# Score tiles of 40 columns, Wo products that may run as column pairs, and a new order of TensorE's pieces

## The chip, the core and the metric

One core of a Trainium2 chip runs the whole program. The metric is device time in microseconds (us), the median of several executions. Three executions of the kernel before took 2647.1, 2651.34 and 2651.9 us.

## What is computed

Two layers in turn, each an attention with a recurrent memory (A) and a gated feed-forward (B), on 2048 tokens of width 576:

```python
x = x + A(layernorm(x)); x = x + B(layernorm(x))     # layer 0
x = x + A(layernorm(x)); x = x + B(layernorm(x))     # layer 1, the same weights

# A: 64 segments of 32 tokens; the 8 memory rows come from the segment before
h = concatenate([mem, xs])                 # 40 x 576
q, k, v = h @ Wq, h @ Wk, h @ Wv           # 32 heads of 128
p = softmax(where(mask, q @ k.T * scale, -1e9))   # 40 x 40 for each head
o = concat_heads(p @ v) @ Wo               # 40 x 576
mem = o[:8]; out = o[8:]

# B
out = (silu(x @ w1) * (x @ w3)) @ w2       # hidden width 4608
```

## The kernel before

The weights of A stay in SBUF. The program walks through 72 steps. In step t, layer 0 works on segment t and layer 1 on segment t-8, so in most steps (56 of 72) each product of A streams 80 columns, 40 for each layer; in the steps at the two ends only one layer is there, and 40 columns are streamed. The feed-forward of a group of four segments is spread over the following four steps, since A alone is a chain from one segment to the next.

`make_nodes` writes all this down as pieces ("nodes"), and `plan` puts them in order. A step has four groups of eight heads. For each group stand, in order of what they need: QK and QKt (the projections to q and k; QKt is the tail of the contraction, 64 rows), SC (scores), the softmax on VectorE and ScalarE, TR (the probabilities transposed, by a DMA where two layers are there), PV (probabilities times V), OTe (its result copied to OT), WO (OT times Wo, four blocks of 128 output columns for each head: 32 products) and WOt (the last 64 columns: 8 products). VG and VGt make V. FF and FFt are w1 and w3, W2 and W2b are w2.

The order of the pieces on TensorE (PE) is a string of letters, `FIRST + FOUR * 11 + LAST` (S is SC, O is WO, o is WOt, and so on); `FOUR` holds four steps and stands eleven times. The other engines' orders follow from due times.

Each piece has a way to use the array of 128 x 128: "full", "col" (products with 64 or 40 output rows, two side by side in the two halves of the columns), "row" (contraction of 64, two above each other), and narrower strips for some of V. A piece may allow several ways, written "full/col". `plan` keeps the way of the piece before as long as the new piece allows it, and counts a change of way otherwise (about 0.096 in its table). Where a "full/col" piece falls into a column stretch, `mm` (line 729's helper) writes each of its products as two with 64 output rows:

```python
def mm(self, out, lhsT, rhs, start, stop, **k):
    if self.mode == "col" and "tile_position" not in k:
        for r in (0, R64):
            self.mm(out[r:r + R64], lhsT[:, r:r + R64], rhs, start, stop, tile_position=(0, r), **k)
        return
```

Each product is a weight load (LDWEIGHTS, PEld in the profile) and a MATMUL. In `scores`, a group with two layers has eight products for the first layer in one half of the columns and eight for the second in the other. The first layer's use 64 columns of weights (40 of its own and 24 of the neighbour), the second's 40.

Of the kernel before, what the change touches and what calls it, by code (L numbers as in the profile page):

```python
# [13 lines left out]
P = 128  # L14
R64 = 64
# [6 lines left out]
QW = SEG + MEM  # L22
# [45 lines left out]
def role(t):  # L68

    return (t - LAG) % 2  # L70
# [152 lines left out]
def ew(*ns):  # L223
    return (actc(*ns), dve(*ns))


def ewh(*ns):
# [2 lines left out]


FIRST = (
    "maqqQQQqSSvxVTXTqPQPSXSOOTPooOoTxPOoQqQSqqqSQQSSvTTVPTPOPoOTOPooOoQqqQvSSVqQQSqSTTPPOOoToTPaPOOooQqvqqSQVSQTQSqx"
    "PTSOPXOTToPoPOOooQqqpvSQVSnqQFFTSfqfPTQFOSPWTFOPoffTOPFOoooWQqfqQSFSVvqfqQQFTTSWPPFSOOxffXToFPWoTfOPFOooFQfqfqQS"
    "VqqvSQQSWTFSPTFfPOTOoPfWTOPFOoooFQffqqQSWQSqVvTSFfQqfWFSTafPFPOToWPTOPOOooobQqqqpQQQxSnXFvqfVSFfqqQQFfqSQPWQqfOS"
    "FPXxWOooPffFFPOOooWQQQqqfqFSFqfqQQQSFqqqfQQWFggfSGSGPGPgfFOOoPWGgfOPFOoooWFqqfQQFSqfqQQQSFvfqqQVSqWqQQfPPSFfOOWP"
    "FOfoFPaooOoWQQqqqqQSQQbSqqqQGSgQqPQGggSPGGPgOOOoPooOoQqqvpQpQQnSqqVqnSQFffqFQQPQqqfSFSOPWwfFOooFPfOWPwfFOooFqqfq"
    "QQQSqqqQQQSWwFfGSFqqfgQQPwWgSGFPGgfOOPWgfGFOoPOoooaqqQQQQqqwFfSSVvQQqqfFWSPwFqfqQQPFSwfOWOFPffFOwWoPOoooFfqqqQQW"
    "SQQqqqQSbQGSgqqQPQGSgOPGggOPGwOoPooOo"
)  # L240
FOUR = (
    "QqqqppQQvVSnnQFqfqqQQSFSFfqfqQQwWPFfPOOSWFoPowffFFPOOoowWQQfqfqFSFfqqqQQwQWSFgfqqQGQPQqgfSWSGFPOwoGggGPOPOOoooaF"
    "qfqqQQQSFqqqfQQQwWvSSVFPQFffqqQOPSWwoffFOPFOwPWOoooFqfqqQQWQSQqqqQQSwSbQQqgqgGSGPGPOoggGPOPOOooo"
)
LAST = (
    "QqqqppQQQqSvVSnnQQqqfFSqqQPQFSffOPFOwPWFOfFoPoofOoWQQQqqqwSQFQqqfGSqgQQPQqfSFGgqgPGSWwfFOFPOfgGOwoPOoooqqqQQQQqS"
    "WFfSVvqfqQFQQPWSwFqfqfQPFOSwWOPFffFOWwoPOoooFqqfqQQQSQFQqqfqQSVSvqqQQWwfSPFVvPWOwPOOobPooxOoXqpQpQqqvVSnSnQFFSTf"
    "fqPTQFSwFPWOTTffPOPOOooooFqffqQQSwFWSQvVqqQTSFPSTWPwFOTffTPOPOOoooowFWvxXVfqQQqfqSQSFFfqSQTwTSWPPFOffTOPFWTOFPwO"
    "ooooFfqfqQQSFSQwfqqQSWSVvTTFwWPffFPOTOTPWPOOoooowbqqpQQxvSSnXVFQfqqQTSTFfSPFPOwTOPFffooTOPFOoowQfqqqQSQSFvVTSQqf"
    "XPFSTwPOTffFPOTFPOOoooofxQfqqQSFSvVwTQqqFSffQwPTSFTPFPOffOTOPwOooooFQqQSqqvVSQQSqwTTSFPFPOoTOoTPffPOOoopfwfFFnFw"  # L250
    "fffFFFwffFFwfffFFwFwfffFFFwffFFwffFFwfffFFww"
)
ORDER = FIRST + FOUR * 11 + LAST

# [1 line left out]
class Opt:  # L256

    qk, qkt, sc, tr, pv, wo, wog, vm = 0.0079, -0.0342, 0.0268, 0.1447, 0.0406, 0.2653, 0.0725, 0.1407
# [4 lines left out]
def make_nodes(em, nseg, pools, o=Opt, dma_bw=230e3, load_bw=380e3, tail_bw=330e3):  # L263
# [4 lines left out]
    def node(*a, **k):  # L268
        n = Node(*a, **k)
        n.prio += 1e-9 * len(nodes)  # L270
        nodes.append(n)
        return n

    def banks(n=2):
        return [Slot("bank") for _ in range(n)]
# [7 lines left out]
    def both(t):  # L283

        return len(layers_of(t - role(t))) == 2


    def load(name, nbytes, prio, fn, deps=()):
        return node("DMA", nbytes / (tail_bw if name == "tail" else load_bw), fn, deps=deps, prio=prio, name=name, lat=2.0)
# [6 lines left out]
    ld_o = [load("ldo", kb(n * E, 576), g - 6.0, em.load_o(g)) for g, (_, n) in enumerate(GROUPS)]  # L296
# [93 lines left out]
    def step(t):  # L390
        ls = layers_of(t)
        nl = 2 if both(t) else 1
# [4 lines left out]
        mm80 = max(c80 / 2.4 + 2.7, 25.1) / 1000  # L397
# [13 lines left out]
        for g, (h0, nh) in enumerate(GROUPS):  # L411
            qs, qe = [], []
            for uh, un in units(g, nl):
# [4 lines left out]
                if pre:  # L418
                    xl.append(node("DMA", 0.5, em.xq_load(t, uh, q), deps=[v[0] for v in [kept_qk.get((t // 4, uh // 4))] if v] + last_qk[-BACK:][:1], prio=pq - 0.3, acq=[q], lat=2.6, name="XL", ring=1.3))
                m_ = node("PE", 8 * un * mmq, em.qk(t, uh, un, b), deps=hx + hm[:1] + ([ld_h[g]] if t == 0 else []),  # L420
                          prio=pq, mode="full", acq=[q] + b, name="QK")
                last_qk.append(m_)
                n = node("PE", un * mmq, em.qk_tail(t, uh, un, b), deps=hx + hm + ([ld_h[g]] if t == 0 else []), prio=pq + o.qkt, mode="row",
                         acq=[q] + b, name="QKt")
                rd += [m_, n]
                me.setdefault(f"QK{g}", []).extend([m_, n])
                for r in (0, 1):
# [4 lines left out]
            s = banks(1)[0]  # L432
            sme = Slot("sme")
            pf = t + o.gstep * h0 / 8
            w40 = nh * QW
            sc = node("PE", nh * (0.0155 * nl if nl == 2 else 0.0255), em.scores(t, g, qs, s), deps=qe, prio=pf + o.sc, mode="col" if nl == 2 else "full/col",
                      acq=[s, sme], rel=[q for q, _, _ in qs], name="SC")
            a = node("DVE", dve(w40), em.sm_add(t, g, s, sme), deps=[sc], prio=pf, rel=[s], name="add")
            m_ = node("DVE", dve(w40, w40) + 0.13, em.sm_max(t, g, sme), deps=[a], prio=pf, name="maxsub")
# [14 lines left out]
            if paired(t):  # L454
                hn = [ht_ready[li, s] for s in (t + 1, t + 2) for li in (0, 1) if (li, s) in ht_ready]
                for blk in blks:
                    if blk // 2 not in vgs:
# [4 lines left out]
            ot = [Slot("ot") for _ in range(nl)]  # L462
            pv = node("PE", nh * mm80, em.pv(t, g, pts, b), deps=pe_ + [d for blk in blks for d in vx_ev["VM", t, blk] + vx_ev["VX", t - e, blk]],
                      prio=pf + o.pv, mode="full/col", acq=b + ot, rel=[pts], name="PV")
            pvs[t, g] = pv
            if paired(t):
                for blk in blks:
                    gb, gd = vgs[blk // 2]
                    vx_ev["VX", t + 1, blk] = vg_out(t, blk, gb, gd + [pv], 0)
            ote = [node("AD", ew(w40), em.ot_ev(t, g, ab, b[ab], ot[ab]), deps=[pv], prio=pf, rel=[b[ab]], name="OTe") for ab in range(nl)]  # L470
            wo = node("PE", 4 * nh * mm80, em.wo(t, g, ot), deps=ote + ([ld_o[g]] if t == 0 else []), prio=t + o.wo + o.wog * h0 / 8, mode="full",
                      acq=[y] if g == 0 else [], name="WO")
            wot = node("PE", nh / 2 * mm80 + (0.013 if nl == 2 else 0.04), em.wo_tail(t, g, ot), deps=[wo], prio=t + o.wo + o.wog * h0 / 8, mode="col", rel=ot[g == NG - 1:], name="WOt")
            if g:
# [11 lines left out]
        if nxt:  # L486
            m = 8 * len(nxt)
# [191 lines left out]
    for t in range(nst):  # L679
        if t % 4 == 2 and (t + 2) // 4 < ngrp:  # L680
            x_in((t + 2) // 4)
        if t == LAG:
            ht_mem[t].append(node("DVE", 0.1, em.init_mem(1, LAG), deps=[m0e] + reads_ht.get(LAG - R_HT, []), prio=LAG - 2, name="m0"))
        if role(t) == 0 or t == 0:
            vx_pair(t - role(t), t - 1 + o.vx)
        step(t)
        if t % 4 == 1 and t // 4 < ngrp:
            x_res(t // 4)
        if t % 4 == 3:
            job((t + 1) // 4 - 1)  # L690
        elif t == nst - 1:
            job(nst // 4)
# [12 lines left out]
class Emitter:  # L705
# [482 lines left out]
    def scores(self, t, g, qs, s):  # L1188

        def f(n):  # L1190
            nh = GROUPS[g][1]
            S = self.bk(s)[:, 0:nh * QW].rearrange("p (h k) -> p h k", h=nh)
            both = self.both(t)
            w = QW * self.nl(t)
            for i in range(max(un for _, _, un in qs)):
                for q, j0, un in qs:
                    if i >= un:
                        continue
                    Q = self.T.QKT[:, q.i]
                    for kd in ((0, 1) if both else (0,)):  # L1200
                        m = (R64 if kd == 0 else QW) if both else P if n.mode == "full" else QW
                        q0 = i * w + (QW * (kd ^ role(t)) if both else 0)
                        self.mm(S[64 * kd:64 * kd + m, j0 + i, :], Q[:, q0:q0 + m], Q[:, un * w + q0:un * w + q0 + QW],
                                True, True, **({"tile_position": (0, 64 * kd)} if n.mode == "col" else {}))
        return f
# [414 lines left out]
```

## Time and profile before

| what | value |
|---|---|
| three executions | 2647.1, 2651.34, 2651.9 us |
| span of the profiled execution | 2659.8 us |
| mean granted TensorE clock | 0.990 |
| instruction count of the profiled execution | 132,078 |
| DMA moved | 371.41 MB |

The profiled execution's own span is 8.5 us (0.3%) above the median of the three. Times inside the program, such as "1450.34", are microseconds from the start of that span. In rows of the timeline the first number is the start, the second the length from the first start to the last end, and "x32" the number of merged instructions; in rows of groups the number behind the bar is the group's share of the engine's busy time in us, and the next the mean length of one instruction in ns. Matmuls overlap in the pipeline, so that length is longer than the distance from one to the next.

### The profile page before, as it was taken

How to read it: one execution, taken by the hardware profiler on the slowest of the kernel's cores; microseconds unless marked ns; L12 is line 12 of the kernel's file. 1: busy time of each engine (PE TensorE's matmuls, PEld its weight loads, DVE VectorE, ACT ScalarE, POOL GpSimd, SP SyncE). 2: the span in 40 equal slices, each digit the busy share in tenths (PEclk: the TensorE clock that was granted, in tenths of full speed). 3: DMA queues.
4: the chain of work that ended last, by engine and by line, in shares of the span. 5: the costliest groups of instructions: out<-in, count | busy, mean ns of one | idle time of the engine just before them, and what ended most of it. 6: DMA issues, size and time to landing. Idle time of an engine off the chain costs nothing.

```text
span 2659.8 us, 132078 instructions
## 1 busy us (share of the span) xinstructions
PE 2571.8 (97%) x58776; PEld 2214.4 (83%) x58818; DVE 2045.3 (77%) x5137; ACT 1225.1 (46%) x3495; POOL 336.9 (13%) x399
## 2 busy tenths in 40 slices
PE   5899999999999999999999999999999999999998
PEld 4778887888888888888888888888888888888887
DVE  4777777777878778788777878877787788778876
ACT  2545453444545354454535444453544445344453
POOL 1111111011101111010111111011110111011110
PEclk8899999999999999999999999999999999999999
DMA  9045746565554655545465555546555554554457
GB/s 317 9 144 155 188 99 142 125 145 146 106 141 115 164 135 147 134 118 139 113 156 126 150 130 129 132 113 152 126 151 133 136 137 105 121 148 120 132 162 246
DMA packets 690428, 371.41 MB, mean 140 GB/s; under 512 B 234328, under 2 KB 682592, under 8 KB 689216
## 3 DMA queue, kind: packets, MB, share of 16 engines
q1 hardware_dynamic: 686320, 355.08, 52.6%
q8 instruction: 460, 7.54, 1.2%
q0 software_dynamic: 3024, 6.93, 1.0%
q10 hardware_dynamic: 512, 0.94, 0.1%
q14 instruction: 112, 0.92, 0.1%
HBM read 306.72 MB, written 2.36 MB: 116 GB/s over the span
## 4 chain that ended last, share of the span: by engine, by line
PE 85%; DMA 6%; DVE 5%; issue 1%; ACT 1%; SPq 0%; ACTq 0%; POOL 0%; DVEq 0%; POOLq 0%
PE bank L729 85%; DMA PTS<-PB 2%; DMA W<-in_B_w_dram 2%; DVE STAT L735 1%; DVE V L735 1%; DVE SME L735 1%; DVE PB L735 1%; DMA W<-in_A_Wq_dram 1%; DMA WO<-in_A_Wo_dram 0%; DMA W<-in_A_Wk_dram 0%; DVE HTT L735 0%; ACT V L732 0%; DVE XR L735 0%; DMA WV<-in_A_Wv_dram 0%; SPq L738 0%
## 5 line engine op out<-in xcount | busy, mean ns | idle before, releaser
L729 PEld LDWEIGHTS <-W 128*128 128x128 bf16 (+2 forms) x31872 | 1258.3, 100 | 150.0 <-issue 72.7
L729 PE MATMUL bank<-HT,W 128*128 128x80 bf16 (+3 forms) x23040 | 796.8, 197 | 23.6 <-issue 8.7
L729 PE MATMUL bank<-XTB,W 128*64 128x256 bf16 (+5 forms) x8832 | 667.4, 263 | 9.2 <-DMA W<-in_B_w_dram 5.8
L1264 POOL MEMSET PB<- 128x1024 bf16 x288 | 273.3, 953 | 1764.3 <-DMA PTS<-PB 1066.0
L732 ACT ACTIVATE QKT<-bank 128x128 bf16<-128x128 f32 (+2 forms) x1497 | 356.0, 316 | 276.9 <-PE bank L729 269.2
L729 PE MATMUL bank<-OT,WO 128*128 128x80 bf16 (+3 forms) x11520 | 414.3, 199 | 5.9 <-ACT OT L732 3.1
L729 PEld LDWEIGHTS <-WO 128*128 128x128 bf16 (+1 forms) x11520 | 385.9, 102 | 22.9 <-issue 10.8
L732 ACT ACTIVATE V<-bank 32x512 bf16<-32x512 f32 (+1 forms) x563 | 319.7, 585 | 174.5 <-PE bank L729 163.1
L729 PE MATMUL bank<-WV,HT 128*32 128x512 bf16 (+4 forms) x3735 | 366.0, 387 | 9.2 <-DMA WV<-in_A_Wv_dram 4.4
L729 PE MATMUL bank<-W2C,HTT 128*64 128x288 bf16 (+1 forms) x3136 | 317.2, 287 | 0.2 <-DMA W2C<-in_B_w_dram 0.2
L732 ACT ACTIVATE HTT<-bank 128x512 bf16<-128x512 f32 (+1 forms) x324 | 176.0, 550 | 277.9 <-PE bank L729 275.4
L735 DVE TENSOR_REDUCE STAT<-SME 104x8 f32<-104x320 f32 (+1 forms) x576 | 274.8, 477 | 29.9 <-ACT SME L732 20.3
L735 DVE TENSOR_TENSOR PB<-SME,STAT 40x128 bf16<-40x128 f32 (+4 forms) x912 | 275.3, 336 | 12.0 <-POOL PB L1264 1.0
L729 PEld LDWEIGHTS <-HT 128*32 128x32 bf16 (+5 forms) x3776 | 157.8, 101 | 139.6 <-issue 42.4
L735 DVE SCALAR_TENSOR_TENSOR HTT<-HTT,bank 128x512 bf16<-128x512 bf16 (+1 forms) x324 | 201.6, 622 | 82.3 <-ACT HTT L732 78.8
L732 ACT ACTIVATE SME<-SME 104x320 f32<-104x320 f32 (+1 forms) x288 | 135.5, 471 | 280.6 <-DVE SME L735 276.9
L729 PEld LDWEIGHTS <-HTT 128*64 128x64 bf16 (+1 forms) x3216 | 232.2, 105 | 32.6 <-issue 1.2
L735 DVE SCALAR_TENSOR_TENSOR XR<-bank,XR 128x288 f32<-128x288 f32 x574 | 240.6, 448 | 16.2 <-PE bank L729 11.8
L732 ACT ACTIVATE OT<-bank 128x320 bf16<-128x320 f32 (+2 forms) x430 | 164.1, 401 | 184.9 <-PE bank L729 171.9
L735 DVE CAST V<-bank 64x512 bf16<-64x512 f32 (+1 forms) x301 | 206.4, 686 | 43.4 <-PE bank L729 35.6
L735 DVE TENSOR_TENSOR HTT<-HTT,bank 128x512 bf16<-128x512 bf16 (+1 forms) x324 | 203.6, 628 | 28.1 <-PE bank L729 0.5
L735 DVE CAST QKT<-bank 128x192 bf16<-128x192 f32 (+4 forms) x423 | 124.4, 335 | 114.3 <-PE bank L729 111.3
(59 smaller groups left out, 1396.5 us busy)
## 6 DMA issues: line engine op xcount, KB each, us to landing
W<-in_B_w_dram SPq DMA_DIRECT2D x608, 256.0 KB, 3.7
W2C<-in_B_w_dram SPq DMA_DIRECT2D x304, 288.0 KB, 3.4
W<-in_B_w_dram SPq DMA_DIRECT2D x608, 32.0 KB, 3.3
W<-in_B_w_dram SPq DMA_DIRECT2D x16, 512.0 KB, 7.3
WO<-in_A_Wo_dram SPq DMA_DIRECT2D x4, 1152.0 KB, 9.8
XR<-in_A_x_dram POOLq DMA_DIRECT2D x16, 288.0 KB, 3.0
WV<-in_B_w_dram SPq DMA_DIRECT2D x8, 576.0 KB, 6.5
W<-in_A_Wq_dram SPq DMA_DIRECT2D x16, 256.0 KB, 7.1
```

The costliest lines, as they stand in the source:

```text
L729: self.ch("PE", self.nc.tensor.matmul(out, lhsT=lhsT, rhs=rhs, start=start, stop=stop, skip_group_check=True, **k))
L732: self.ch("ACT", self.nc.scalar.activation(*a, **k))
L735: self.ch("DVE", getattr(self.nc.vector, fn_)(*a, **k))
L1264: return lambda n: self.ch("POOL", self.nc.gpsimd.memset(self.T.PB[:, pb.i, 0:GROUPS[g][1]], 0.0))
```

## The change

Three edits, none of which changes what is computed.

1. `scores`: both layers' products use 40 columns of weights. The planner's figure for a group falls from 0.0155 to 0.0126 for each head and layer.
2. WO allows "full/col" in place of "full" where two layers are there.
3. `FIRST`, `FOUR` and `LAST` are new strings with the same letters in each in another order (a line of `FOUR` is shown).

```diff
@@ -230,25 +230,25 @@
 FOUR = (
-    "QqqqppQQvVSnnQFqfqqQQSFSFfqfqQQwWPFfPOOSWFoPowffFFPOOoowWQQfqfqFSFfqqqQQwQWSFgfqqQGQPQqgfSWSGFPOwoGggGPOPOOoooaF"
+    "QqqqppQQVvnSnQFqqqfQQSFSFfqqfQQPWFwSffPOFOwWooffFPFPOOoowQQQqqqqSQWSFfqqqQQQQFqfgfFSGwWPFgfSGGPOoggwOPGWPOOoooFq"
...
@@ -433,7 +433,7 @@
-            sc = node("PE", nh * (0.0155 * nl if nl == 2 else 0.0255), em.scores(t, g, qs, s), deps=qe, prio=pf + o.sc, mode="col" if nl == 2 else "full/col",
+            sc = node("PE", nh * (0.0126 * nl if nl == 2 else 0.0255), em.scores(t, g, qs, s), deps=qe, prio=pf + o.sc, mode="col" if nl == 2 else "full/col",
...
@@ -468,7 +468,7 @@
-            wo = node("PE", 4 * nh * mm80, em.wo(t, g, ot), deps=ote + ([ld_o[g]] if t == 0 else []), prio=t + o.wo + o.wog * h0 / 8, mode="full",
+            wo = node("PE", 4 * nh * mm80, em.wo(t, g, ot), deps=ote + ([ld_o[g]] if t == 0 else []), prio=t + o.wo + o.wog * h0 / 8, mode="full/col" if nl == 2 else "full",
...
@@ -1198,7 +1198,7 @@
-                        m = (R64 if kd == 0 else QW) if both else P if n.mode == "full" else QW
+                        m = P if n.mode == "full" and not both else QW
```

Counted over the whole program, the pieces and their products are the same, but more of them run in column pairs: of the 7,168 full WO products with 80 columns 480 are left, and 13,376 halves stand for the others. PV has 336 full products in place of 1,256, w2 616 in place of 1,328, w1 and w3 2,032 in place of 2,976 (with 256 columns). In all PE has 9,423 matmuls more, each with its weight load, 68,241 in place of 58,818. One copy of `FOUR` has 3,994 matmuls in place of 3,314. The way of using the array changes 1,097 times over the program, before 1,171 times.

The first place is on PE, in the middle of the program, where the scores of a group begin (QKT is q and k of the group, W and HT the projection ahead of it, W2C and HTT a w2 product ahead of it). Before:

```order
L729 LDWEIGHTS W
L729 MATMUL bank_92<-HT,W 128x80
L729 LDWEIGHTS QKT
L729 MATMUL bank_89<-QKT 64x40
L729 LDWEIGHTS QKT
L729 MATMUL bank_89<-QKT 40x40
L729 LDWEIGHTS QKT
L729 MATMUL bank_89<-QKT 64x40
```

And in the changed kernel:

```order
L729 LDWEIGHTS HTT
L729 MATMUL bank_87<-W2C,HTT 128x288
L729 LDWEIGHTS QKT
L729 MATMUL bank_90<-QKT 40x40
L729 LDWEIGHTS QKT
L729 MATMUL bank_90<-QKT 40x40
L729 LDWEIGHTS QKT
L729 MATMUL bank_90<-QKT 40x40
```

The number of products is the same; the ones with 64 output rows are gone.

The second place is on PE too, where WO follows a PV in column pairs. Before:

```order
L729 MATMUL bank_92<-PTS,V 64x80
L729 LDWEIGHTS V
L729 MATMUL bank_92<-PTS,V 64x80
L729 LDWEIGHTS WO
L729 MATMUL bank_90<-OT,WO 128x80
L729 LDWEIGHTS WO
L729 MATMUL bank_90<-OT,WO 128x80
```

And in the changed kernel:

```order
L729 MATMUL bank_90<-PTS,V 64x80
L729 LDWEIGHTS V
L729 MATMUL bank_90<-PTS,V 64x80
L729 LDWEIGHTS WO
L729 MATMUL bank_86<-OT,WO 64x80
L729 LDWEIGHTS WO
L729 MATMUL bank_86<-OT,WO 64x80
L729 LDWEIGHTS WO
L729 MATMUL bank_86<-OT,WO 64x80
```

The array stays in column pairs through WO, and WO takes twice as many instructions.

More of the change, by code (lines that the diff above doesn't have):

```diff
@@ L232 @@
 FIRST = (
[L233 to L237, printed above, removed]
@@ L238 @@
-    "QQQSqqqQQQSWwFfGSFqqfgQQPwWgSGFPGgfOOPWgfGFOoPOoooaqqQQQQqqwFfSSVvQQqqfFWSPwFqfqQQPFSwfOWOFPffFOwWoPOoooFfqqqQQW"
-    "SQQqqqQSbQGSgqqQPQGSgOPGggOPGwOoPooOo"
+    "maQqqQqQSSvxXVSQTPqTPSXTxPOTOOPoooOoQqQSqqSQQSqvTTSVPTPOPOTOPoooOoQqvqSQVqSQQSqSTTPPOTOPTooPOOooaQqvqSQVqSQQSTqP"
+    "TSXPOOTooTPxPOOooQpQqqVnSSvqfFFQQSTTfqPFfOPFSOoTWoPffFTOPFOooWQfqqQSVfvSFqQQfTqTSPXPSOoWTOPoFfTOPFOooxWQqqfFSQVv"
+    "QSFfqqTQSWSTFPFPOTOPffooOToWPFOofFQfqQSWFqqfQvSSVqTWFQffTPSPFTOaPoWTOPOOooobQpQQqqqQnSvqfFSFQfqVQxqXFSWQqfqPQfFS"
@@ L240 @@
+    "POoxfXOWFPfFPOOoooWQqqfqFQQSQqqqfFSQQGSFqfgqQQPFGgfSWgGPOfFPOgFGoOPoOofWoFQQfqqQqqfSFQQvSWVqfFQqqQFSPQqWSfaOPfoO"
+    "oWFPfFOPoOoWQQqqqqQSbqQQQqSGSgQQqqGSgPGPOoggOPGOPooOoVppqQQqqqQQnnSSvfFQFqqfQQQqqfSFPFSfPwOWOooFffFPwOPWOofoFFqq"
+    "fqQQwQSQQQqgqqGWSFSfPQFQfqqgGSGgPOOgPGWooOoPwOoFqfqQwWQVSfqvFQQQqqwFSfqWPQQQSFqfqFOSPWwfOooFfPFOowfPWOoFqqfQQWqq"
+    "aSQQQqqSbQQQqgqSGgSwPGGPOggGoPOPOoOoo"
 )
 FOUR = (
-    "QqqqppQQvVSnnQFqfqqQQSFSFfqfqQQwWPFfPOOSWFoPowffFFPOOoowWQQfqfqFSFfqqqQQwQWSFgfqqQGQPQqgfSWSGFPOwoGggGPOPOOoooaF"
@@ L243 @@
-    "qfqqQQQSFqqqfQQQwWvSSVFPQFffqqQOPSWwoffFOPFOwPWOoooFqfqqQQWQSQqqqQQSwSbQQqgqgGSGPGPOoggGPOPOOooo"
+    "QqqqppQQVvnSnQFqqqfQQSFSFfqqfQQPWFwSffPOFOwWooffFPFPOOoowQQQqqqqQSWSFfqqqQQQQFqfgfFSGwWPFgfSGGPOoggwOPGWPOOoooFq"
+    "fqqQQWQwSQQqqfqQvSFSVFPQQqqffFOPSWOwooFffFPwOPoWOoFqqfqQQQSaWqqqQQQSwbSQQqqgGSGPgGPOggOoPGOPooOo"
 )
 LAST = (
-    "QqqqppQQQqSvVSnnQQqqfFSqqQPQFSffOPFOwPWFOfFoPoofOoWQQQqqqwSQFQqqfGSqgQQPQqfSFGgqgPGSWwfFOFPOfgGOwoPOoooqqqQQQQqS"
-    "WFfSVvqfqQFQQPWSwFqfqfQPFOSwWOPFffFOWwoPOoooFqqfqQQQSQFQqqfqQSVSvqqQQWwfSPFVvPWOwPOOobPooxOoXqpQpQqqvVSnSnQFFSTf"
@@ L248 @@
[L248 to L251, printed above, removed]
+    "QqqqppQQQSqqqQQSnnvVqfQSFQqfPFOSFPWfOowfFPFPOOooowQQqqfWQSQqfqFSQQgqfqFGSqQPQqggGwWSGPFPOgfGoOwoPOFOooWFqffqQQQq"
@@ new lines @@
+    "qwSWQQQqfqSFSVvFPQQqqffFSOWfFPowPOFffOPFOoWoowQQQqqqFSfqQQfqqSQWQqqQSwSvVFPPVOovWOPwoOPboOoVpQpqqQSqnvxQnSXqFTSQ"
+    "PFTSffOTFPFPOTwPOffOoWooFoFqqffQQwSWvqVSQTQPSwqfFSTOTPWFFPTOPOfxXOwooooWQqfqfQSFQSFfqfVvqTSFPQTWwSOPTffFFPWTwOPO"
+    "OooooFqfQWQSFqfvQwSqTVqfSFQWTwSPFfTPOPOWoTowPOOoboQqqqpSvQQSVSTnQFfqXTxfFPFPTSOPOOoooffwTFPFOoffQqqwQFSQVqvSwFQS"
+    "TqfXfPTFSPOFTOPowfTOPooOoxQqqqQSFSfvVfQFSQTwPfqTFFTSPOPOOfoooTfwPFOoQqQSqVqvqSQwQSTFSPTFPOOoToffTPPOOoowfpFfFnwf"
+    "ffFFFFwffFFwfffFFwFwfffFFFwffFFwffFFwfffFFww"
```

## The prediction

> **What bounds the kernel now.** First the page's busy times and its chain of work that ended last, then PE's waits, then the middle of the program in three stretches (the columns behind the length are busy us and counts of PE, PEld, DVE, ACT and POOL, the granted clock, the DMA share and GB/s):
>
> ```profile
> span 2659.8 us, 132078 instructions
> PE 2571.8 (97%) x58776; PEld 2214.4 (83%) x58818; DVE 2045.3 (77%) x5137; ACT 1225.1 (46%) x3495; POOL 336.9 (13%) x399
> ...
> PE 85%; DMA 6%; DVE 5%; issue 1%; ACT 1%; SPq 0%; ACTq 0%; POOL 0%; DVEq 0%; POOLq 0%
> ```
>
> ```profile
> PE bank L729 <- issue: 16.6, 41, 1.4
> PE bank L729 <- DMA PTS<-PB: 12.4, 12, 2.5
> ```
>
> ```profile
> 300.00:1000.00 700.00, 686.54 (x14988) 589.49 (x14999) 547.03 (x1373) 324.09 (x964) 85.94 (x100) 1.00 0.56 133
> 1000.00:1700.00 700.00, 692.78 (x15062) 600.32 (x15074) 552.34 (x1366) 323.96 (x965) 85.78 (x99) 1.00 0.55 135
> 1700.00:2400.00 700.00, 689.55 (x15123) 595.98 (x15131) 549.99 (x1373) 327.13 (x964) 85.87 (x100) 1.00 0.54 131
> ```
>
> PE is the bound: 97% of the span, 85% of the chain, and in the 2100 us of the middle it is idle for only 2100 - 2068.9 = 31 us. So what shortens PE's work shortens the kernel, as long as PE gets its instructions and its data. The largest of its waits is "issue", 16.6 us in 41 gaps: no semaphore ends those. The middle runs 45,173 matmuls in 2100 us, one in 46.5 ns.
>
> **The score tiles.** The timeline shows one group of scores; behind it the other half of the array already goes on with V's products:
>
> ```profile
> 1450.34 0.37 PE L729 MATMUL bank<-QKT 128*64 128x40 bf16 x15
> 1450.55 0.38 PE L729 MATMUL bank<-WV,HT 128*64 128x512 bf16 x1
> 1450.56 0.19 PE L729 MATMUL bank<-QKT 128*64 128x40 bf16 x1
> ...
> 2600.95 3.18 PE L729 MATMUL bank<-HT,W 128*128 128x40 bf16 x121
> ```
>
> The last score product starts 0.22 us after the first, seven steps on its half, so 31 ns a step. The half with 40 columns was through with its eight steps after 0.21 us, 26 ns each; the row of 121 full products of 40 columns has 26 ns too (3.18/121). With 40 columns on both halves each group should save 8 x 5 to 6 ns, some 0.045 us. There are 56 x 4 = 224 such groups: **-10 us**. The bounds are 0, if the lag of one half is lost in what follows anyway, and -13 (8 x 7 ns). I take -10, since the next products do start late on the lagging half.
>
> **The changes of way.** A PV in column pairs followed by a full WO:
>
> ```profile
> 1454.29 0.59 PE L729 MATMUL bank<-PTS,V 128*64 128x80 bf16 x16
> 1454.82 1.58 PE L729 MATMUL bank<-OT,WO 128*128 128x80 bf16 x40
> ...
> 1458.89 1.31 PE L729 MATMUL bank<-OT,WO 128*128 128x80 bf16 x32
> ```
>
> ```profile
> L729 PE MATMUL bank<-OT,WO 128*128 128x80 bf16 x7168 | 285.8, 202 | 2.0 <-ACT OT L732 1.9
> L729 PE MATMUL bank<-OT,WO 128*64 128x80 bf16 x1792 | 57.3, 204 | 0.0
> ```
>
> A product lasts 202 ns, so the last of PV starts at 1454.29 + 0.59 - 0.20 = 1454.68, and WO 0.14 us later. Within WO the distance is (1.31 - 0.20)/31 = 36 ns. A change of way costs about 0.10 us. There are 74 fewer: **-7 us**, between 0 (if they were hidden in waits) and -8.
>
> **WO and others as column pairs.** What a pair costs is in a row where two groups' full WO and two tails in column pairs are merged, and in rows of the feed-forward:
>
> ```profile
> 1501.82 2.87 PE L729 MATMUL bank<-OT,WO 128*128 128x80 bf16 x80
> ...
> 1499.79 1.91 PE L729 MATMUL bank<-XTB,W 128*128 128x256 bf16 x16
> 1509.81 1.94 PE L729 MATMUL bank<-XTB,W 128*64 128x256 bf16 x32
> ```
>
> Of the 2.87 us, 64 full ones take 64 x 36 = 2.30, the change 0.10 and the last one's length 0.20; 0.27 is left for the 16 halves: 17 ns each, 34 a pair, like one full product's 36. In w1 and w3, 16 full ones take 1.91 and 32 halves 1.94. So a pair is priced like the product it replaces, **0 us**; the change of 10 us or less that 6,688 pairs at 1.5 ns would make either way stays in the range. The dearest reading is the group's busy time: 57.3/1792 = 32 ns for a half, 64 for a pair, against 285.8/7168 = 40, which would be +24 ns x 6,688 = 161 us; it holds the changes of way and starts of all those short tails, so it is far too high.
>
> The weight load of a full tile and of a half take about the same time in this trace: 0.27 us for 16 halves, loads included. [...]
>
> **The fetch of instructions.** Twice the instructions for the same work must be brought in. The page's queue of instructions, and the end of the program, where the gaps named "issue" are dense:
>
> ```profile
> q8 instruction: 460, 7.54, 1.2%
> ```
>
> ```profile
> 2592.30 1.05 PE L729 MATMUL bank<-XTB,W 128*64 128x128 bf16 x31 [0.56 <-issue]
> 2593.29 2.59 PE L729 MATMUL bank<-HT,W 128*128 128x40 bf16 x97
> 2596.60 1.33 PE L729 MATMUL bank<-HT,W 128*128 128x40 bf16 x47 [0.72 <-issue]
> ...
> 84.48 3.96 PE L729 MATMUL bank<-HT,W 128*128 128x40 bf16 x160 [0.32 <-ACT HT L732]
> ```
>
> 7.54 MB in 460 packets is 16.4 kB each; 117,594 loads and matmuls in 460 make 256 a packet, 128 matmuls with their loads. And between the two gaps stand exactly 31 + 97 = 128 matmuls, 4.30 us from gap to gap, of which 0.72 was waited. So a packet comes in about 4 us, and PE stands where 128 matmuls are done sooner. In the row at 84.48, though, 128 of 160 matmuls take 128/160 x 3.96 = 3.2 us without a gap: the next packet is under way before a stretch begins, so a short stretch behind a longer one goes free.
>
> In the middle 128 matmuls take 128 x 46.5 ns = 5.95 us on the mean; with 3,994 for 3,314 it will be 4.9. A column PV, two groups of WO and two tails in a row (16 + 64 + 64 + 8 + 8 halves of 18 ns) take 2.9 us for 160 matmuls. I priced the whole listing by rows like those above and cut it in packets. Before, 39 of 458 stretches of 128 take less than 4.0 us, short by 19.5 us in all, near the 16.6 of the waits, and nearly all at the two ends of the program. In the changed kernel it is 133 of 531, short by 80, most of it in the middle. If a packet is asked for some 20 matmuls ahead, stretches of about 150 count: 14 before, short by 4, and 53 after, short by 24. So the cost is between +20 and +60 us by 4.0 us, and +8 if the packet comes in 3.5. I take **+11**, near the low end, because the dense spots in the middle are single ones between w1, w3 and w2 products, as in the row at 84.48. What hides the rest is the longer stretch ahead; without that cover it is +60. A stall holds everything behind it on PE, and the copies of ScalarE and VectorE after it.
>
> [...]
>
> **Waits on data.** The new order moves every piece, and no row prices that: 0, within 5 us either way, a sixth of the 31 us that PE idles in the middle. VectorE has 36 instructions more of 5,139 and ScalarE 36 fewer of 3,501: nothing. VectorE still adds and reduces the same 104 rows. Loads and stores stay.
>
> **Sum.** -10 - 7 + 0 + 11 + 0 = -6 us on the span of 2659.8; on the median of the runs, 2651.3: **2645 us**.
>
> **The rivals.**
> Rival 1, the fetch takes it all: growth of more than 22 us, slower. For it: a mean of 4.9 us for 128 matmuls leaves little above 4.0, and packets won't all come equally fast. Against it: the cover at 84.48. It decides from 22 us on (17 gained, 5 for the band); at +40 the time is 2674, at +60 it is 2694.
> Rival 2, gains and fetch cancel: growth of 12 to 22 us, 2651. The two counts allow it fully.
> Rival 3, pairs are dearer than priced, or the new order waits more for data. 5 ns a pair of WO are 33 us: 2678. The row of 80 speaks against it, but it has only sixteen halves in a row, never sixty-four.
>
> **How the numbers follow.** The forecast has 0.43, rival 2 0.20, rival 1 0.27, rival 3 0.10. A measurement tells changes from about 0.2% (5 us). Faster 0.43, same 0.20, slower 0.37. The forecast's own range is 2630 to 2646; the range for 8 in 10 takes in rival 2 and half of rival 1: low end with fetch at 0, scores at -12 and waits at -5, 2627; high end with fetch at +50, 2684.
>
> **What would show it.** Right: the score groups' last product starts 0.18 us after the first; a WO in column pairs lasts 1.3 us like the full one; packets rise to 533; "issue" grows by 8 to 15 us. Wrong: "issue" gaps of half a microsecond and more in the middle, 128 matmuls apart, right behind WO; or WO pairs wider than 36 ns; or more waits for PTS, OT or HT.

## The result, and the profile after

The changed kernel takes 2681.66 us (median of four, 2679.61 to 2683.47), the kernel before 2649.47 beside it: ratio 1.0124, 95% interval 1.0110 to 1.0138. It is 32 us slower. The forecast was 6 us faster, 2645; the time lies just inside the range of 2627 to 2684, on rival 1's side.

The page after, busy times, chain and the queue of instructions:

```profile
span 2681.2 us, 151023 instructions
PE 2570.1 (96%) x68226; PEld 2210.3 (82%) x68241; DVE 2052.5 (77%) x5173; ACT 1223.2 (46%) x3459; POOL 337.1 (13%) x399
...
q8 instruction: 533, 8.73, 1.3%
...
PE 82%; DVE 8%; DMA 5%; issue 3%; ACT 1%; SPq 0%; POOL 0%; ACTq 0%; DVEq 0%; POOLq 0%
```

PE's busy time is the same to 2 us with 9,423 more matmuls, and packets of instructions rose from 460 to 533, as worked out. The chain's share of "issue" rose from 1% to 3%. PE's waits over the whole program, then the same view for the middle alone (300 to 2400 us; us in total, times, longest), first after:

```profile
PE bank L729 <- issue: 44.0, 66, 2.8
```

```profile
PE bank L729 <- issue: 35.7, 56, 2.8
PE bank L729 <- DVE V L735: 5.8, 11, 0.5
PE bank L729 <- DMA W2C<-in_B_w_dram: 5.6, 6, 1.9
...
PE bank L729 <- DMA PTS<-PB: 2.1, 4, 0.9
```

and before:

```profile
PE bank L729 <- DMA PTS<-PB: 11.8, 11, 2.5
PE bank L729 <- ACT HT L732: 4.5, 13, 0.3
PE bank L729 <- DMA W<-in_B_w_dram: 4.5, 7, 1.1
PE bank L729 <- issue: 3.6, 23, 0.2
```

The waits on data did not grow (in the middle PE idled 27 us for other reasons than "issue" before, 24 after): the one for the transposed probabilities fell from 11.8 to 2.1, VectorE's for V and the one for w2 took some of that back. What grew is "issue", from 3.6 to 35.7 us in the middle. The view hides part of each gap, since the last product before it still counts as busy for its 0.2 us while the next would have started after 0.02 to 0.04.

The whole middle in one row (the columns as in the prediction's), after and before:

```profile
300.00:2400.00 2100.00, 2039.97 (x53832) 1765.70 (x53839) 1634.04 (x4099) 955.50 (x2817) 252.70 (x291) 1.00 0.57 133
```

```profile
300.00:2400.00 2100.00, 2068.87 (x45163) 1785.79 (x45199) 1649.37 (x4111) 975.17 (x2892) 257.58 (x299) 1.00 0.55 133
```

PE idles 60 us of the 2100, before 31, and 128 matmuls take 5.0 us on the mean. VectorE and ScalarE did less in the same 2100 us, since the slower program gets less far in them.

The timeline after shows where PE stands, behind PV and two groups of WO:

```profile
572.60 0.45 PE L729 MATMUL bank<-PTS,V 128*64 128x80 bf16 x16
572.88 1.50 PE L729 MATMUL bank<-OT,WO 128*64 128x80 bf16 x74
575.02 1.45 PE L729 MATMUL bank<-OT,WO 128*64 128x80 bf16 x70 [0.64 <-issue]
576.26 1.18 PE L729 MATMUL bank<-W2C,HTT 128*64 128x288 bf16 x16
577.38 1.68 PE L729 MATMUL bank<-HT,W 128*128 128x80 bf16 x42
579.86 4.03 PE L729 MATMUL bank<-HT,W 128*128 128x80 bf16 x118 [0.81 <-issue]
```

From gap to gap stand 70 + 16 + 42 = 128 matmuls, one packet (2 x 68,241 loads and matmuls in 533 packets are 256 each), 4.84 us. The first gap lies inside WO, the second among the full products of a projection: the pairs use up the packets, and whoever comes next stands too. The chain's view names only the pieces; the count of 128 is what tells this stall from a wait.

Three terms of the sum can be read off as well. The scores of a group, and two groups of WO, after:

```profile
1500.73 0.38 PE L729 MATMUL bank<-QKT 128*40 128x40 bf16 x16
...
1501.92 1.32 PE L729 MATMUL bank<-OT,WO 128*64 128x80 bf16 x64
1503.07 1.92 PE L729 MATMUL bank<-XTB,W 128*64 128x256 bf16 x32
1504.82 1.31 PE L729 MATMUL bank<-OT,WO 128*64 128x80 bf16 x64
```

The sixteen score products start within 0.38 - 0.18 = 0.20 us (a product lasts 0.18), where 0.18 was forecast and 0.22 stood there before; in e1's row below it is 0.36 - 0.18 = 0.18, 26 ns a step on each half (before, 31 on one). A WO in 64 halves lasts 1.31 to 1.32 us, like 32 full products before (1.31). So the pair is priced right, and the scores too.

### The profile page after: what moved, and what is told of

It reads as the page before. It is cut to its first block, busy times and chain, and to the rows that moved or that the text cites. A ratio compares the mean times of both kernels' runs of the same rounds, so it can differ in the third digit from the quotient of the medians.

```text
span 2681.2 us, 151023 instructions
## 1 busy us (share of the span) xinstructions
PE 2570.1 (96%) x68226; PEld 2210.3 (82%) x68241; DVE 2052.5 (77%) x5173; ACT 1223.2 (46%) x3459; POOL 337.1 (13%) x399
## 4 chain that ended last, share of the span: by engine, by line
PE 82%; DVE 8%; DMA 5%; issue 3%; ACT 1%; SPq 0%; POOL 0%; ACTq 0%; DVEq 0%; POOLq 0%
PE bank L729 82%; DVE V L735 2%; DMA W2C<-in_B_w_dram 2%; DMA PTS<-PB 1%; DVE STAT L735 1%; DVE SME L735 1%; DVE LNS L735 1%; DMA WV<-in_A_Wv_dram 1%; DMA W<-in_B_w_dram 1%; DVE PB L735 1%; DVE XR L735 1%; DMA W<-in_A_Wq_dram 0%; ACT V L732 0%; DVE HTT L735 0%; POOL LNS L940 0%
## 5 line engine op out<-in xcount | busy, mean ns | idle before, releaser
L729 PE MATMUL bank<-HT,W 128*128 128x80 bf16 (+3 forms) x23040 | 785.9, 197 | 24.2 <-issue 6.4
L732 ACT ACTIVATE QKT<-bank 128x64 bf16<-128x64 f32 (+4 forms) x1462 | 349.2, 319 | 311.9 <-PE bank L729 304.1
L729 PE MATMUL bank<-OT,WO 128*64 128x80 bf16 (+3 forms) x18208 | 415.1, 200 | 25.0 <-issue 21.8
L729 PEld LDWEIGHTS <-WO 128*64 128x64 bf16 (+1 forms) x18208 | 393.4, 111 | 44.6 <-issue 36.3
L729 PE MATMUL bank<-W2C,HTT 128*64 128x288 bf16 (+1 forms) x3848 | 323.2, 288 | 10.5 <-DMA W2C<-in_B_w_dram 5.6
L729 PEld LDWEIGHTS <-HTT 128*64 128x64 bf16 (+1 forms) x3928 | 238.0, 108 | 48.2 <-issue 18.4
L729 PEld LDWEIGHTS <-HT 128*32 128x32 bf16 (+4 forms) x3992 | 148.6, 102 | 140.1 <-issue 29.0
L732 ACT ACTIVATE OT<-bank 128x320 bf16<-128x320 f32 (+2 forms) x409 | 157.7, 400 | 166.3 <-PE bank L729 157.9
L735 DVE CAST QKT<-bank 128x128 bf16<-128x128 f32 (+2 forms) x458 | 130.5, 329 | 122.6 <-PE bank L729 119.4
```

The source lines that it names most:

```text
L729: self.ch("PE", self.nc.tensor.matmul(out, lhsT=lhsT, rhs=rhs, start=start, stop=stop, skip_group_check=True, **k))
L732: self.ch("ACT", self.nc.scalar.activation(*a, **k))
L735: self.ch("DVE", getattr(self.nc.vector, fn_)(*a, **k))
```

## The experiments

The kernels were timed in four groups, each beside the kernel before, which took 2649.5, 2655.3, 2659.2 and 2654.7 us there. So kernels of different groups are compared by their ratios to it.

**e1: the scores alone.** In the kernel before, with nothing else changed:

```diff
-                        m = (R64 if kd == 0 else QW) if both else P if n.mode == "full" else QW
+                        m = P if n.mode == "full" and not both else QW
```

> Before with both halves' score products at 40 columns, the order and the planner's figures untouched. The prediction's term: 224 groups x 0.045 us come off, about 2639 us, 10 below before. Rival: the old order was laid out so that what follows the scores starts when its data is there, and the saved time turns into waits on data: within 3 us of before.

Measured: 2648.7 beside 2655.3, ratio 0.9976 (0.9964 to 0.9987): 6.4 us faster (3.5 to 9.6), between the two. The group in its timeline:

```profile
1498.74 0.36 PE L729 MATMUL bank<-QKT 128*40 128x40 bf16 x16
1498.94 2.24 PE L729 MATMUL bank<-XTB,W 128*64 128x256 bf16 x36
```

The next products start 0.20 us after the first score product, as priced. In the two profiled executions PE's busy time falls by 9.9 us, from 2571.8 to 2561.9, which is the whole term, and PE idles no longer than before (84 us, before 88). So the third of the 10 us that the medians lack is not seen in the profiles, and the interval nearly reaches 10; whether it is lost, and where, stays open.

**e2: WO held to full products.** In the changed kernel:

```diff
-            wo = node(..., mode="full/col" if nl == 2 else "full",
+            wo = node(..., mode="full",
```

> The changed kernel with WO held to full products; order string, 40-column scores and all else as changed. 58,809 matmuls, as many as before (58,818). Fetch theory: the gaps named issue fall from 44 us to under 20, and the time falls by 35 to 45 us, to about 2640, in spite of the changes of way that come back. Rival, the new order waits more for data: it stays near 2675. Rival, the pairs themselves are dear: it falls as well, but the gaps named issue are about as long as in the changed kernel.

Measured: ratio 0.9988 (0.9978 to 0.9997), and timed again (e9) 0.9999 (0.9989 to 1.0008), beside the changed kernel's 1.0125 on the same chip: 2654.6 against 2686.4, 32 us, just under the 35 to 45 expected; by the ratios of the first times, 1.0124 and 0.9988, it is 36. PE's waits over the whole program:

```profile
PE bank L729 <- DMA XTB<-in_A_mem_dram: 10.7, 1, 10.7
PE bank L729 <- issue: 8.1, 12, 1.1
PE bank L729 <- ACT HT L732: 7.0, 19, 0.7
```

"issue" falls from 44.0 to 8.1 us, less than the 16.6 of the kernel before, and in the middle none is left. So the new order is not what is slow. It is no gain either: with the same scores and full WO the old order (e1, 0.9976) is some 3 to 6 us faster. The way of using the array changes 1,324 times in this kernel and 1,097 times in the changed one. By the 0.10 us of the prediction the pairs save 23 us of PE's work in this order, and cost 32 all the same: by this estimate the fetch takes back some 55.

**e5: pairs in the old order.** The kernel before with 40-column scores, the new figure for them, and

```diff
-            wo = node(..., mode="full",
+            wo = node(..., mode="full/col" if nl == 2 else "full",
```

> Before with 40-column scores and WO allowed as column pairs, in the old order (and the planner's new figure for scores): 67,330 matmuls. Fetch theory: dense stretches as in the changed kernel, 50 to 65 us of stalls, 2670 to 2685, so not the new order but the pairs make it slow. Rival, the new order is at fault and pairs are free: 2640 to 2646 by the changes of way saved.

Measured: 2706.6 beside 2655.3, ratio 1.0195 (1.0174 to 1.0216), slower than the changed kernel:

```profile
PE bank L729 <- issue: 60.3, 77, 2.2
PE bank L729 <- DMA PTS<-PB: 20.3, 18, 4.3
```

So pairs make it slow in either order, and the new order makes it less slow than the old one; why was not tested. It is 51 us slower, where 20 to 35 was expected (2670 to 2685 against 2649.5). "issue" grew by 44 us (60.3, before 16.6), and the wait for the transposed probabilities by 8, from 12.4 to 20.3.

**e3: more instructions, but not dense.** In the kernel before, the full products of w1, w3 and w2 and all main products of VG are written as two of half the streamed columns; for w1 and w3:

```diff
+                            if n.mode == "full" and hi - lo == 2 * P:
+                                for hb in (0, 1):
+                                    o_ = slice(fb * 2 * P + hb * P, fb * 2 * P + (hb + 1) * P)
+                                    self.mm(self.bk(b[r])[:, o_], W[:, 4 * r + c, fs], self.T.XTB[:, hb, c, :], first and fb == 0 and c == 0 and hb == 0,
+                                            fb == 1 and c == 3)
+                                continue
```

> Before with the full products of w1, w3 and w2 and all of VG each written as two of half the streamed columns: 63,578 matmuls in place of 58,818, half of what the change added, but where a product is long. By the rows of the profile a split costs about 2.5 ns for each product: about +10 us. Fetch theory: these stretches stay well over 4 us for 128 matmuls, so 2657 to 2664 and issue under 22 us. Rival, the number of instructions costs as such: half of the change's 42 us of stalls on top, 2675 to 2685.

Measured: 2675.4 beside 2655.3, ratio 1.0072 (1.0058 to 1.0086), 20 us slower. As a time that is in the rival's range; against the kernel before it lies between the two, which were 8 to 15 and 26 to 36 us above 2649.5. The profile decides it. The middle, and PE's busy time and waits over the program:

```profile
300.00:2400.00 2100.00, 2075.71 (x49177) 1913.96 (x49178) 1640.98 (x4091) 967.80 (x2877) 255.68 (x297) 1.00 0.56 133
```

```profile
PE 2587.4 (97%) x63578; PEld 2363.7 (88%) x63578; DVE 2046.1 (77%) x5137; ACT 1225.0 (46%) x3495; POOL 336.2 (13%) x399
```

```profile
PE bank L729 <- issue: 20.2, 24, 2.2
PE bank L729 <- DMA PTS<-PB: 11.8, 10, 2.4
```

The middle runs 4,000 matmuls more than before, PE is idle there for 24 us in place of 31, and its waits there show no "issue" at all. All 20.2 us lie at the ends, where the kernel before has 13.0 of its 16.6. PE's work rose by 15.6 us, 3.3 ns for each of the 4,760 splits: I had priced the split too low, at 2.5. So the 20 us are PE's work and some 7 us of stalls at the ends. In the middle, more instructions as such brought no stall; where they stand decides.

**e4: the fetch by itself.** Behind the last piece of the kernel before:

```diff
+    def halves(m):
+        for i in range(m // 2):
+            for r in (0, R64):
+                em.mm(k[r:r + R64, 0:80], T.WO[:, 0, r:r + R64], T.OT[:, 0, 0:80], True, True, tile_position=(0, r))
+    def wide(m):
+        for i in range(m):
+            em.mm(k[:], T.WO[:, 0, 0:P], T.WO[:, 1, 0:512], True, True)
+    em.mode = None
+    wide(24)
+    halves(1280)
+    for m in (64, 96, 128, 160, 192, 256):
+        for i in range(6):
+            wide(28 + 3 * i)
+            halves(m)
+    wide(24)
```

> Before, with dummy products added behind its last piece: 1,280 halves like WO's pairs in one run, then for each length of 64, 96, 128, 160, 192 and 256 six bursts of such halves, each behind 28 to 43 full products of 512 columns; the result does not use them. All other work is done by then. Fetch theory: a half alone takes 18 ns, 128 of them 2.3 us, but the long run goes at the pace of the packets, 3.5 to 4.3 us for 128 halves and 35 to 43 us for the run, with gaps 128 matmuls apart; bursts of 64 never stand, bursts of 160 or more mostly do. Rival, pairs run at their own pace: 23 us for the run and no gaps.

The long run in the timeline (one execution, 3085.8 us in all with the added work):

```profile
2662.77 2.48 PE L729 MATMUL bank<-OT,WO 128*64 128x80 bf16 x128 [1.53 <-issue]
2666.24 2.48 PE L729 MATMUL bank<-OT,WO 128*64 128x80 bf16 x128 [0.99 <-issue]
2669.71 2.48 PE L729 MATMUL bank<-OT,WO 128*64 128x80 bf16 x128 [0.99 <-issue]
2673.73 2.48 PE L729 MATMUL bank<-OT,WO 128*64 128x80 bf16 x128 [1.53 <-issue]
2677.48 2.48 PE L729 MATMUL bank<-OT,WO 128*64 128x80 bf16 x128 [1.26 <-issue]
2681.50 2.48 PE L729 MATMUL bank<-OT,WO 128*64 128x80 bf16 x128 [1.53 <-issue]
```

128 halves start within 2.3 us, and then PE stands until the next packet is there: 3.47 to 4.02 us from packet to packet, 3.75 on the mean of these five, with no other transfer under way. The whole run of 1,280 halves takes 36.0 us (2653.99 to 2689.97). Of the bursts, those of 64, 96 and 128 halves never stood, of 160 one in six, of 192 two, of 256 five. One of 192 and one of 256:

```profile
2956.00 3.06 PE L729 MATMUL bank<-OT,WO 128*64 128x80 bf16 x160
2959.43 0.77 PE L729 MATMUL bank<-OT,WO 128*64 128x80 bf16 x32 [0.36 <-issue]
...
3042.59 3.17 PE L729 MATMUL bank<-OT,WO 128*64 128x80 bf16 x166
3046.57 1.80 PE L729 MATMUL bank<-OT,WO 128*64 128x80 bf16 x90 [0.81 <-issue]
```

The long run went as expected. The cover for one burst is better than I wrote there (160 "mostly do" was wrong): a packet and a quarter of dense halves went free in five of six bursts, behind 6 us or more of long products. If the places where a packet ends are carried on in steps of 128 matmuls from the long run's gaps, all eight bursts that stood did so at the second such place that they came to, and none at the first; two that began 2 and 12 matmuls ahead of one ran over their second as well. By these eight gaps a burst got through the rest of the packet that it began in and the whole next one (157 to 254 halves), and where it began in the first decided how far it got.

**e6: the change with 64-column scores.** The changed kernel with e1's edit undone.

> The changed kernel with the first layer's score products back at 64 columns; all else as changed. By the prediction's term 10 us come back, 2690. By e1, where the same edit gave 6 us in the old order, 2686 to 2690. Rival: where PE stands for instructions, the 50 ns of a group are lost in the next gap, within 4 us of the changed kernel.

Measured: ratio 1.0151 (1.0134 to 1.0168) against the changed kernel's 1.0124 and 1.0125, some 7 us; the intervals overlap. "issue" is 43.0 us there and 44.0 and 50.9 in the changed kernel. It goes with e1's 6 us; it does not rule out the rival.

**e7 to e9: pairs where the packets allow them.** In the changed kernel, with e8 (the change) and e9 (e2) beside it:

```diff
+PAIRS = ((0, 0, 0, 0), (0, 0, 0, 1), (0, 1, 1, 0), (0, 1, 1, 0))
...
-            wo = node(..., mode="full/col" if nl == 2 else "full",
+            wo = node(..., mode="full/col" if nl == 2 and PAIRS[t % 4][g] else "full",
```

> The changed kernel with WO allowed as pairs in five of the sixteen groups of four steps (step 1 group 3, step 2 groups 1 and 2, step 3 groups 1 and 2), chosen so that the packets there keep above 4 us; 57 of 288 WO run as pairs, 61,377 matmuls. Fetch theory: gaps named issue in the middle under 8 us (35.7 in the changed kernel), and fewer changes of way than with full WO, so 3 to 10 us below e2 and below before as well, ratio to before 0.993 to 0.998. Rival, any pairs in WO cost a share of the 36 us between e2 and the changed kernel, 57 of 209: 10 us above e2, ratio 1.002.

> The changed kernel as it is, beside the others on one chip: ratio to before 1.011 to 1.014, issue 40 to 48 us.

> The kernel of e2 as it is, beside the others on one chip: ratio to before 0.998 to 1.0.

Measured: e7 0.9973 (0.9964 to 0.9983), 2647.7 us beside 2654.7; e8 1.0125 (1.0102 to 1.0147); e9 0.9999 (0.9989 to 1.0008). The changed kernel's "issue" was 50.9 us this time, above the 40 to 48 expected. e7's waits in the middle (the helper's line is 730 there):

```profile
PE bank L730 <- issue: 1.5, 3, 0.7
PE bank L730 <- DMA PTS<-PB: 0.8, 2, 0.6
```

57 of the WO groups run as pairs and bring 1.5 us of "issue" in the middle; the rival's 1.002 is ruled out. e7 beats both kernels by 7 us and 39 us. It does no better than e1, the old order with only the scores changed.

## Why the prediction was wrong, point by point

- **The score tiles, -10 us.** The mechanism held: both halves step in 26 ns (e1), and PE's busy time fell by 9.9 us there. In time it was worth 6.4 us alone (e1), and about 7 in the new order (e6), not clear of noise.
- **The changes of way, -7 us.** Not measured by themselves. Between e2 and the changed kernel there are 227 of them, and e7 gains 7 us over e9 with 82 fewer, which is 0.085 us each (0.04 to 0.13 by the intervals); the 0.10 taken lies in that.
- **The pairs' own price, 0 us.** Held: 1.31 us for 64 halves, as for 32 full products, though a load of WO for a half took 113 ns on the mean and for a full tile 99 (before). The first half of rival 3, dearer pairs, fell with the 1.31 us; its second, more waits on data, fell too.
- **The fetch, +11 us.** This is the step that failed, by its size. The prediction named the mechanism, counted 133 short packets in place of 39, worked out +20 to +60 at 4.0 us a packet, and then took +11, "near the low end, because the dense spots in the middle are single ones", going below its own low count by way of a packet of 3.5. What is left of the 32 us after the gains is 32 + 7 + 6 = 45. By e2 it is much the same: some 55 there, less the 8 us by which "issue" in e2 lies below the kernel before, 47. Of it "issue" shows 27 as idle time, with up to 0.18 us of each gap not shown. With that, the 56 gaps of the middle come to some 46 us (35.7 + 56 x 0.18, an estimate), and the ends have some 6 less than before, so about 40 of the 45 stand in the gaps; the rest hangs on the two gains as priced. Three things stood in its place. In e4 a packet came in 3.47 to 4.02 us with nothing else moving, so 3.5 was its best there and not its usual time. PV, WO, WO and two tails are 160 halves in a row, at the edge of what one burst had free in e4 (160 in five of six), with row pairs and scores soon behind. And the spots return in each copy of four steps, at other places of the packet (3,994 matmuls are 31 packets and 26 matmuls).
- **The sum.** With e2's +47 for +11 and the scores at -6 it ends at 2649.5 - 6 - 7 + 47 = 2683 (measured 2681.7). That closes the account and does not test it, since the 47 is worked out from much the same 32 us. Rival 1, which had 0.27, gave 2674 for a growth of 40.
- What would show it wrong was named rightly: gaps in the middle, 128 matmuls apart, in and right behind WO.

## What to carry to other kernels

Before more and smaller instructions are set in place of fewer ones, cut the listing into the fetch's packets and ask what the shortest packets take, not the mean: here 5.0 us on the mean was fast enough and the dense ones, 128 halves in 2.3 us (e4), were not. When a count gives a range for a cost, take the number from inside the range; a single row that shows the best case (here one run of products without a gap) is no reason to go below it. A planner that sees only PE's own prices will trade a 0.1 us change of way for 32 more products, each with its weight load; e7 shows that the trade is good where a packet is long anyway: 2647.7 us beside e9's 2654.6, with 1.5 us of "issue" in the middle.

## What the hardware showed beside that

In e4's long run the transfer of a packet was the smaller part of its 3.47 to 4.02 us. There (2662.5 to 2690 us) the instruction queue is the only one with packets, and its share of 16 engines' time is

```profile
q8 instruction: 7, 0.11, 2.0%
```

which is 1.26 us for each of the seven. By the trace's packet times they took 0.93 to 1.43 us. Each started when 58 to 64 matmuls of the 128 at hand had started, so when half a packet was left and not the last "some 20 matmuls" that the prediction supposed, and PE went on 1.2 to 1.6 us after it had landed. The gaps of the long run in e4 take few values, 0.99, 1.26 and 1.53 us, 0.27 apart; the two of 0.99 follow the shortest packets (0.93 and 0.96 us), why the values are so few was not tested. In the changed kernel single gaps reach 2.8 us. Ahead of the longest, with weights of the feed-forward under way, the packet took 2.54 us, where the median in the middle is 1.03, and PE went on 1.6 us after it had landed.
